# Moving an integer addition from GpSimd to VectorE, and twelve subtractions the other way, in the weight conversion of a fused attention and two-layer kernel

## The chip, the cores and the metric

One NeuronCore of a Trainium2 chip runs the whole program in one launch. The metric is device time in microseconds (us) for one execution, the median of several executions. The engines are TensorE (PE for its matmuls, PEld for its weight loads), VectorE (DVE), ScalarE (ACT), GpSimd (POOL) and SyncE (SP), whose queue issues most of the DMAs.

## The reference

For 8 batches and 8 heads, keys and values are averaged over groups of 8 positions (576 positions become 72), and q (576 x 64 for each head) attends to them. The result, 4608 tokens of 512, passes through two layers. Everything is float32, but the weights arrive as float64.

```
k_p = k.reshape(B, H, S // 8, 8, D).mean(axis=3);  v_p = v.reshape(B, H, S // 8, 8, D).mean(axis=3)
attn = softmax(q @ k_p.T / sqrt(D));  x = attn @ v_p          # 4608 x 512
x = ((x @ w1) * (x @ w2)) @ w3 @ w_out                        # 512 -> 1024 -> 1024 -> 512
h = x @ w_in;  out = (h * sigmoid(1.702 h)) @ w_out2          # 512 -> 2048 -> 512
```

## The kernel before, in words

**Precision.** TensorE works on float32 tiles that are split in two: a rounded part ("hi", a copy by ScalarE, L104) and the rest ("lo", the difference of the value and hi, L105). `split` (L103) makes both; its argument `lo_eng` names the engine of the subtraction, VectorE or GpSimd. Each product is made by three matmuls (`mm3`, L114 to L116): hi by hi, hi by lo, lo by hi.

**Weight conversion.** A float64 weight chunk of 128 x 512 values is loaded as pairs of 32-bit words (512 KB, SP queue, L151). The class `Conv` turns a chunk into float32. `load` (L146) keeps up to nine loaded chunks staged, as slots come free. `step` (L155) takes one: ScalarE turns the high words into `e` (L166) and the low words into small integers (L168, in place), VectorE shifts `e` left by three bits into the tile `cv` (L169), and GpSimd adds the small integers to it as 32-bit integers (L172). Then the slot of the loaded chunk is given back. A line of two further places lets a chunk be used one or two steps later: `turn` transposes w3's chunks on TensorE (L508, into PSUM), and `done` splits the float32 chunk into a slot. `Conv.to` (L139) is `done` for w_out, w1 and w2; without an engine its subtraction goes to GpSimd (L142). w3's chunks are split from PSUM by VectorE (L515).

**First part of the program** (some 110 us). w3 @ w_out is multiplied beforehand, so that the first layer has one matrix in their place. The loop at L568 makes 28 conversion steps: 8 chunks of w_out and 16 of w3, and the first chunks of w1 and w2. Beside them run `w3_mm` (the products, accumulated in PSUM tiles `acc`) and `tick`, which makes one step of the attention of one pair of heads: the transposes of k and q on VectorE (L255, L256), the scores on TensorE (L278), maxima, exponents and sums (L283 to L303: among them L301, an addition of a constant to 128 x 10 values, and L303, the multiplication of 128 x 720 exponents), further transposes (L314 on VectorE), and pooled values and subtractions on GpSimd (L324 to L372). L391 subtracts for the lo part of the attention's output.

**Second part**: nine blocks of 512 tokens (L602), each with eight chunks of 128 hidden values. For each, 24 matmuls make the two products with w1 and w2 in the PSUM tiles `wk`, L638 and L641 (L644 in the last two blocks) multiply them, the product is split, and `x2_step` (L585) multiplies earlier chunks with the combined matrix. Two ticks of attention run in each chunk of seven of the blocks. In the first block the rest of w1 and w2 is converted; in the last two blocks w_in and w_out2 are converted (32 chunks; `e` lies in PSUM here, L616), split by `units` (L463), and written to DRAM.

**Third part** (from about 760 us): the second layer, its weights streamed from DRAM. No conversion runs there.

The order of the instructions on an engine isn't that of the program text: the framework's scheduler sets it when the program is built (`schedule_with_timeline_sim=True` in the launch). Each engine then takes its own list in order, with semaphores between engines.

The change touches `step` at L172, the loop at L551 that names the engine for w_out's chunks (VectorE for the even ones), and L561, which names VectorE for w2's chunks. w1's chunks go to GpSimd already (L559).

Of the kernel before, what the change touches and what calls it, by code (L numbers as in the profile page):

```python
# [22 lines left out]
def pooled_attention_moe_moe2(  # L23
# [18 lines left out]
    nc = tc.nc  # L42
# [6 lines left out]
    w1, w2, w3, w_out, w_in2, w_out2 = (w.bitcast(U32) for w in (w1, w2, w3, w_out, w_in2, w_out2))  # L49
# [45 lines left out]
    def give(*ts):  # L95
        for t in ts:
            if id(t) in held:
                free.append(held.pop(id(t))[1:])
# [19 lines left out]
    def col_tile(w, f):  # L118
        return w[:, 2 * f * P:2 * (f + 1) * P].rearrange("(c p) m -> p c m", p=P)

    def row_tile(w, f):
        return w[f * P:(f + 1) * P, :]
# [4 lines left out]
    class Conv:  # L127
# [27 lines left out]
        def step(self):  # L155

            new = None
            if self.staged:
                t, turn, done = self.staged.pop(0)
                lo_w, hi_w = t[:, :, 0], t[:, :, 1]  # L160
                w = cv_p[0].tile([P, T], F32, name="cv", tag="cv", bufs=4)
                wu = w.bitcast(U32)

                e = self.ps[self.n % len(self.ps)] if self.ps else w
                self.n += 1
                nc.scalar.activation(  # L166
                    e, hi_w.bitcast(F32), AF.Prelu, scale=2.0 ** -112, alpha=-2.0 ** 32)
                nc.scalar.activation(lo_w.bitcast(I32), lo_w, AF.Copy, scale=2.0 ** -29)  # L168
                nc.vector.tensor_scalar(  # L169
                    out=wu, in0=e.bitcast(U32), scalar1=3, scalar2=None,  # L170
                    op0=ALU.logical_shift_left)
                nc.gpsimd.tensor_tensor(  # L172
                    out=w.bitcast(I32), in0=w.bitcast(I32), in1=lo_w.bitcast(I32), op=ALU.add)
                give(t)
                new = [w, turn, done]
            mid, old = self.line
            if mid and mid[1]:
                mid[0] = mid[1](mid[0])
            key = old[2](old[0]) if old else None
            self.line = [new, mid]  # L180
            self.load()
            return key
# [4 lines left out]
    conv = Conv()  # L187
# [3 lines left out]
    with pa_ctx:  # L191
# [264 lines left out]
        wo_s, wp_s, w1_s, w2_s = {}, {}, {}, {}  # L456
# [87 lines left out]
        def add_3(it, jh):  # L544
            conv.add(w3[sl(it), 2 * jh * T:2 * (jh + 1) * T], w3_turn(it, jh), w3_done(it, jh))

        for jh in range(2):
            for i in range(4):
                j = jh * 4 + i
                conv.add(row_tile(w_out, j), None,  # L550
                         conv.to(wo_s, j, nc.gpsimd if i % 2 else nc.vector, j,  # L551
                                 j if j < NA else None))
                if i < 2:
                    add_3(i, jh)
# [3 lines left out]
        for f in range(NF1):  # L558
            conv.add(col_tile(w1, f), None,  # L559
                     conv.to(w1_s, f, a=f - FA if 0 <= f - FA < NA else None))  # L560
            conv.add(col_tile(w2, f), None, conv.to(w2_s, f, nc.vector))  # L561

        conv.load()
        g_load(0)
# [564 lines left out]
```

## Time and profile before

| | us |
|---|---|
| median of 3 executions | 1483.03 (1482.06 to 1484.38) |
| the profiled execution | 1482.22 |
| its span in the profile | 1480.3 |
| PE busy in the span | 1437.6 |
| DVE busy | 989.9 |
| ACT busy | 694.3 |
| POOL busy | 491.0 |

The span runs from the first to the last instruction that the profile shows; 1.9 us of the profiled execution lie around it. A busy share is an average over parts of the program with different limits, so the stretches are looked at one by one. "Granted clock" is the share of TensorE's full clock that the chip gave it. A row of a group reads: line, engine, operation, output tile <- input tiles, shapes, count, then the busy time in us and the mean of one instruction in ns, then idle time of the engine just before and what ended it. A row of a stretch reads: from and to, length, then for PE, PEld, DVE, ACT and POOL the busy time and in brackets the count of instructions, then the granted clock, the mean busy share of the 16 DMA engines and their GB/s.

### The profile page before, as it was taken

What the parts mean: (1) busy time and instruction counts of PE and PEld (TensorE: products, weight loads), DVE (VectorE), ACT (ScalarE), POOL (GpSimd) and SP (SyncE); (2) the same over time, 40 slices, a digit from 0 to 9 for tenths busy, and PEclk for the clock granted to TensorE, in tenths of its full rate; (3) what the DMA queues carried; (4) which work ended last, traced back from release to release, by engine and by line L of the source; (5) the groups of instructions that cost most, each with busy time, mean ns of one, the idle gap of its engine ahead of it and who ended that gap; (6) DMA issues with size and microseconds to landing.
All of it is one profiled execution on the core that took longest, in us unless ns stands there. A gap on an engine that the chain in (4) does not pass through costs nothing.

```text
span 1480.3 us, 19432 instructions
## 1 busy us (share of the span) xinstructions
PE 1437.6 (97%) x6536; PEld 1186.8 (80%) x6536; DVE 989.9 (67%) x1728; ACT 694.3 (47%) x1212; POOL 491.0 (33%) x589
## 2 busy tenths in 40 slices
PE   5978999999999999999999999999999999999998
PEld 3757888888888888888888887788788888888886
DVE  7889998878787877645536355693559354944554
ACT  6874444434343434366635335552455244634442
POOL 8787865555555555357743200000000000000000
PEclk8999999999999999999999999999999999999999
DMA  9992333323232321089879979867677766785665
GB/s 273 235 232 45 65 77 65 74 49 75 48 75 49 74 44 38 29 288 339 329 232 384 336 237 314 295 200 228 199 237 224 223 199 217 240 237 181 194 213 139
DMA packets 294435, 267.64 MB, mean 181 GB/s; under 512 B 201664, under 2 KB 226240, under 8 KB 294336
## 3 DMA queue, kind: packets, MB, share of 16 engines
q1 hardware_dynamic: 291648, 265.09, 59.8%
q10 hardware_dynamic: 2688, 1.31, 0.3%
q8 instruction: 52, 0.85, 0.2%
q14 instruction: 47, 0.39, 0.1%
HBM read 209.72 MB, written 56.62 MB: 180 GB/s over the span
## 4 chain that ended last, share of the span: by engine, by line
PE 85%; DVE 6%; DMA 4%; ACT 3%; issue 1%; SPq 0%; POOL 0%; DVEq 0%; ACTq 0%; POOLq 0%
PE bk L709 40%; PE wk L114 9%; PE wk L116 8%; PE wk L115 8%; PE acc L116 4%; PE acc L114 4%; PE acc L115 4%; PE wk L278 2%; DMA wud<-wt 2%; PE bk L115 1%; PE bk L116 1%; PE bk L114 1%; DVE s L105 1%; DVE cv L169 1%; DMA st<-wind 1%
## 5 line engine op out<-in xcount | busy, mean ns | idle before, releaser
L709 PE MATMUL bk<-mv,st 128*128 128x512 f32 x1152 | 271.5, 389 | 1.0 <-ACT mv L104 1.0
L709 PE MATMUL bk<-xM,st 128*128 128x512 f32 x1092 | 258.5, 390 | 3.2 <-ACT u L967 1.3
L709 PEld LDWEIGHTS bk<-mv,st 128*128 128x128 f32 x1152 | 216.1, 188 | 46.4 <-ACT mv L104 1.6
L709 PEld LDWEIGHTS bk<-xM,st 128*128 128x128 f32 x1092 | 204.5, 188 | 47.6 <-issue 2.5
L114 PE MATMUL wk<-s,s 128*128 128x512 f32 x576 | 227.9, 397 | 6.2 <-DVE a L641 3.6
L115 PE MATMUL wk<-s,s 128*128 128x512 f32 x576 | 225.4, 392 | 1.6 <-DVE s L391 1.5
L116 PE MATMUL wk<-s,s 128*128 128x512 f32 x576 | 225.3, 392 | 0.1
L314 DVE STREAM_TRANSPOSE p<-s_t 32x160 f32<-32x160 f32 (+1 forms) x560 | 178.5, 319 | 10.5
L115 PE MATMUL acc<-s,s 128*128 128x512 f32 x352 | 140.3, 399 | 1.2 <-POOL s L105 1.1
L116 PE MATMUL acc<-s,s 128*128 128x512 f32 x352 | 139.8, 397 | 1.6 <-DVE s L105 1.6
L114 PE MATMUL acc<-s,s 128*128 128x512 f32 x352 | 132.4, 402 | 7.4 <-DVE s L105 5.0
L114 PEld LDWEIGHTS wk<-s,s 128*128 128x128 f32 x576 | 108.7, 189 | 30.5 <-DVE a L641 4.7
L115 PEld LDWEIGHTS wk<-s,s 128*128 128x128 f32 x576 | 108.5, 188 | 24.0 <-DVE s L391 2.4
L116 PEld LDWEIGHTS wk<-s,s 128*128 128x128 f32 x576 | 108.5, 188 | 23.1 <-DVE s L105 0.5
L105 POOL TENSOR_TENSOR s<-a,s 128x512 fp32r<-128x512 f32 x56 | 73.4, 1310 | 155.1 <-ACT s L104 121.3
L105 DVE TENSOR_TENSOR mv<-g,mv 128x1024 fp32r<-128x1024 f32 x80 | 97.7, 1221 | 33.4 <-ACT mv L104 32.1
L104 ACT CAST mv<-g 128x1024 fp32r<-128x1024 f32 x80 | 84.3, 1053 | 72.5 <-PE bk L709 72.1
L172 POOL TENSOR_TENSOR cv<-cv,s 128x512 int32<-128x512 int32 x72 | 100.7, 1406 | 35.9 <-DVE cv L169 22.7
L114 PEld LDWEIGHTS acc<-s,s 128*128 128x128 f32 x352 | 67.2, 192 | 22.5 <-ACT s L104 4.6
L116 PEld LDWEIGHTS acc<-s,s 128*128 128x128 f32 x352 | 67.2, 191 | 15.7 <-DVE s L105 2.9
L115 PEld LDWEIGHTS acc<-s,s 128*128 128x128 f32 x352 | 67.3, 191 | 14.5 <-POOL s L105 2.3
L638 ACT COPY a<-wk 128x512 f32<-128x512 f32 x72 | 42.0, 583 | 68.4 <-PE wk L116 68.2
(188 smaller groups left out, 2341.8 us busy)
## 6 DMA issues: line engine op xcount, KB each, us to landing
st<-wud SPq DMA_DIRECT2D x96, 512.0 KB, 4.3
st<-wind SPq DMA_DIRECT2D x66, 512.0 KB, 4.7
st<-wind SPq DMA_DIRECT2D x76, 256.0 KB, 4.0
s<-in_moe_w_dram SPq DMA_DIRECT2D x32, 512.0 KB, 6.5
wind<-s SPq DMA_DIRECT2D x32, 512.0 KB, 5.4
s<-in_moe_w_out_dram SPq DMA_DIRECT2D x24, 512.0 KB, 6.6
kr<-in_k_dram SPq DMA_DIRECT2D x128, 72.0 KB, 2.5
qr<-in_q_dram SPq DMA_DIRECT2D x128, 72.0 KB, 2.5
```

What stands on the lines that cost most here:

```text
L104: nc.scalar.copy(dst[:, 0], src)
L105: lo_eng.tensor_tensor(out=dst[:, 1], in0=src, in1=f32(dst[:, 0]), op=ALU.subtract)
L114: nc.tensor.matmul(o, a[:, 0, a_sl], b[:, 0, b_sl], start=first, stop=False)
L115: nc.tensor.matmul(o, a[:, 0, a_sl], b[:, 1, b_sl], start=False, stop=False)
L116: nc.tensor.matmul(o, a[:, 1, a_sl], b[:, 0, b_sl], start=False, stop=last)
L169: nc.vector.tensor_scalar(out=wu, in0=e.bitcast(U32), scalar1=3, scalar2=None, op0=ALU.logical_shift_left)
L172: nc.gpsimd.tensor_tensor(out=w.bitcast(I32), in0=w.bitcast(I32), in1=lo_w.bitcast(I32), op=ALU.add)
L278: nc.tensor.matmul(sc[half][:, i * KW:(i + 1) * KW], qT[:, sl(tt)], mov, start=True, stop=True)
L314: nc.vector.transpose(out=dst[:, :nt, 32 * c:32 * c + 32], in_=s_t[32 * c:32 * c + 32, :nt, 32 * r:32 * r + 32])
L638: nc.scalar.copy(a, pa_)
L709: nc.tensor.matmul(o, w[:, x, m], b[:, y], start=first and n == 0, stop=last and n == 2, skip_group_check=True)
```

## The change

The addition of a conversion is made by VectorE, right behind its shift. The subtractions for the lo parts of w_out's four even chunks and of w2's eight chunks are made by GpSimd.

```diff
@@ Conv.step
                 nc.vector.tensor_scalar(
                     out=wu, in0=e.bitcast(U32), scalar1=3, scalar2=None,
                     op0=ALU.logical_shift_left)
-                nc.gpsimd.tensor_tensor(
+                nc.vector.tensor_tensor(
                     out=w.bitcast(I32), in0=w.bitcast(I32), in1=lo_w.bitcast(I32), op=ALU.add)
                 give(t)
@@ conv.add of w_out
             conv.add(row_tile(w_out, j), None,
-                         conv.to(wo_s, j, nc.gpsimd if i % 2 else nc.vector, j,
+                         conv.to(wo_s, j, nc.gpsimd, j,
                                  j if j < NA else None))
@@ conv.add of w2
-            conv.add(col_tile(w2, f), None, conv.to(w2_s, f, nc.vector))
+            conv.add(col_tile(w2, f), None, conv.to(w2_s, f))
```

## Rows read from the trace of the kernel before

**Rows 1.** Busy time by stretch: PE, PEld, DVE, ACT, POOL; clock; DMA share; GB/s

```profile
0.00:20.00 20.00, 9.21 (x25) 6.17 (x26) 11.37 (x16) 15.54 (x26) 13.52 (x22) 1.00 0.94 281
20.00:40.00 20.00, 14.27 (x55) 9.39 (x54) 18.60 (x23) 12.27 (x27) 18.68 (x21) 0.74 1.03 272
40.00:80.00 40.00, 38.37 (x218) 31.48 (x216) 33.50 (x59) 36.80 (x78) 28.66 (x30) 1.00 0.96 227
80.00:120.00 40.00, 30.30 (x128) 22.93 (x129) 35.93 (x52) 28.30 (x63) 33.95 (x41) 0.91 0.99 208
120.00:160.00 40.00, 36.44 (x168) 29.69 (x167) 34.00 (x71) 18.71 (x38) 34.17 (x36) 1.00 0.15 32
160.00:620.00 460.00, 459.45 (x2212) 387.50 (x2212) 379.08 (x931) 183.16 (x414) 247.59 (x357) 1.00 0.26 57
620.00:760.00 140.00, 139.97 (x620) 115.49 (x619) 73.07 (x105) 80.01 (x143) 90.84 (x72) 1.00 0.84 299
760.00:1481.00 721.00, 709.58 (x3120) 584.11 (x3118) 404.38 (x477) 319.53 (x425) 23.59 (x16) 1.00 0.74 235
```

**Rows 2.** What PE waited for, 0 to 160 us: total us, times, longest

```profile
PE wk L508 <- POOL cv L172: 10.6, 2, 9.2
PE acc L114 <- DVE s L105: 5.0, 3, 3.0
PE wk L114 <- DVE a L641: 3.6, 2, 1.9
PE wk L278 <- DVE qT L256: 2.8, 2, 2.1
...
PE acc L116 <- DVE s L105: 1.6, 1, 1.6
PE wk L115 <- DVE s L391: 1.5, 1, 1.5
```

**Rows 3.** Groups by line and shape, VectorE, 0 to 160 us

```profile
L169 DVE TENSOR_SCALAR cv<-cv 128x512 uint32<-128x512 uint32 x40 | 30.8, 777 | 10.5 <-ACT cv L166 10.5
L105 DVE TENSOR_TENSOR s<-cv,s 128x512 fp32r<-128x512 f32 x11 | 13.1, 1187 | 1.5 <-ACT s L104 1.5
...
L301 DVE TENSOR_SCALAR nm<-nm 128x10 f32<-128x10 f32 x7 | 8.9, 1271 | 0.1
L303 DVE TENSOR_TENSOR s_t<-s_t,nm 128x720 f32<-128x720 f32 x4 | 8.0, 1988 | 0.1
```

**Rows 4.** Groups by line and shape, GpSimd, 0 to 160 us

```profile
L172 POOL TENSOR_TENSOR cv<-cv,s 128x512 int32<-128x512 int32 x40 | 54.9, 1377 | 17.3 <-DVE cv L169 4.3 <-DMA s<-in_moe_w_dram 3.5 <-DMA kr<-in_k_dram 1.9
L105 POOL TENSOR_TENSOR s<-cv,s 128x512 fp32r<-128x512 f32 x12 | 15.5, 1295 | 3.0 <-ACT s L104 2.8
```

**Rows 5.** Single lines over the whole span: ns min/median/max, first and last start

```profile
L169 DVE TENSOR_SCALAR cv<-cv x40: 357/515/2590, 5.5 to 148.9; 128x512 uint32<-128x512 uint32 x40
...
L301 DVE TENSOR_SCALAR nm<-nm x32: 155/173/3399, 30.8 to 610.8; 128x10 f32<-128x10 f32 x32
...
L303 DVE TENSOR_TENSOR s_t<-s_t,nm x30: 895/899/4380, 33.9 to 611.2; 128x720 f32<-128x720 f32 x30
...
L105 DVE TENSOR_TENSOR s<-cv,s x12: 679/1146/2070, 8.1 to 169.6; 128x512 fp32r<-128x512 f32 x12
```

**Rows 6.** Timeline of GpSimd, 5 to 11 us: start, us, instruction

```profile
7.84 1.30 POOL L172 TENSOR_TENSOR cv<-cv,s 128x512 int32<-128x512 int32 x1 [0.42 <-DVE cv L169]
```

**Rows 7.** Timeline of VectorE, 30 to 36 and 82 to 91 us

```profile
30.75 2.25 DVE L301 TENSOR_SCALAR nm<-nm 128x10 f32<-128x10 f32 x1
...
83.51 3.40 DVE L301 TENSOR_SCALAR nm<-nm 128x10 f32<-128x10 f32 x1
```

**Rows 8.** Timeline of GpSimd, 83 to 88 us

```profile
85.60 1.27 POOL L172 TENSOR_TENSOR cv<-cv,s 128x512 int32<-128x512 int32 x1
```

**Rows 9.** Busy time of line 172 alone (GpSimd), 40 to 80 us

```profile
40.00:80.00 40.00, 14.41 (x11) 1.00 0.96 227
```

**Rows 10.** Groups by line and shape, GpSimd, 620 to 760 us

```profile
L172 POOL TENSOR_TENSOR cv<-cv,s 128x512 int32<-128x512 int32 x32 | 45.7, 1442 | 18.7 <-DVE cv L169 18.4
```

## The prediction, made before the change was run

> **What bounds the kernel now.** I read the stretches first. In each, the reader should subtract PE's busy time from the length: from 160 to 760 us PE is idle for 0.6 us, from 760 on for 11.4 us with no conversion running, and from 0 to 160 us for 31.4 us [rows 1]. All later time is PE's own work, so what the change does from 160 us on is seen only if it makes PE idle there; what it does before 160 us shifts the end one for one. The conversions lie in two places: 40 before 160 us, 32 from 620 to 760 us [rows 4, 10].
>
> Next, the waits of PE before 160 us. VectorE ends five kinds of them, 14.5 us in nine waits; GpSimd's addition ends 10.6 us, of which 9.2 is the start of the program [rows 2]. So VectorE sets the pace more than GpSimd. Both are crowded: VectorE is busy 133.4 of 160 us, GpSimd 129.0, and loads keep the DMA engines at 0.94 to 1.03 until 120 us [rows 1].
>
> Last, what fills VectorE. The shift takes 0.36 us at best and 0.78 on the mean; L301 0.16 against 1.27; L303 0.90 against 1.99; the subtraction from `cv` 0.68 against 1.19 [rows 3, 5]. One L301 of 3.40 us on 128 x 10 values ends at 86.91, 0.04 after a GpSimd addition (85.60 plus 1.27) [rows 7, 8]. I read this as VectorE being held while GpSimd runs. For the 40 shifts the surplus is 30.8 - 40 x 0.36 = 16.4 us, for seven L301 8.9 - 1.1 = 7.8, for four L303 8.0 - 3.6 = 4.4: 28.6 us of VectorE's time are waiting [rows 3, 5].
>
> **The change part by part, up to 160 us.**
>
> *GpSimd* loses 54.9 us of additions and gains twelve subtractions, at 1.295 us each 15.5 us: 129.0 becomes 89.6 us, 81% becomes 56% [rows 1, 4].
>
> *VectorE gains* 40 additions. No row shows one on VectorE; the nearest is the subtraction from `cv`, same size, two SBUF inputs: 0.68 us free, 1.19 us on the mean as now held [rows 3, 5]. I take 0.88, which is 0.68 plus half of the 0.41 that a shift loses now, because GpSimd is less full then: 35.2 us, ends 27.2 and 47.6.
>
> *VectorE loses* eleven subtractions before 160 us, 13.1 us [rows 3]; the twelfth starts at 169.6 [rows 5].
>
> *VectorE is held less.* If the surplus follows GpSimd's busy share, it falls by 30%: 8.7 us. If VectorE must find a gap between GpSimd's instructions, it follows busy over free time (129/31 against 89.6/70.4) and falls by 69%: 19.8 us. The L301 of 3.40 us is longer than any single GpSimd instruction that the groups show (means of 1.3 to 1.4), so it outlasted several; I take the middle, 14.3 us [rows 4, 7].
>
> The Trainium skill ("SBUF — State Buffer", Who interferes with whom) says that the engine which starts first holds the shared port pair for its whole instruction. By that, a wait should end with one GpSimd instruction, the relief would be the 8.7 us, and VectorE would gain 13.4 us where the next sentence has 7.8; the 3.40 us row does not agree.
>
> Net: 35.2 - 13.1 - 14.3 = 7.8 us more on VectorE, ends -5.7 (27.2 - 13.1 - 19.8) and +25.8 (47.6 - 13.1 - 8.7). It has 26.6 us idle in this stretch [rows 1], so most of it needn't show; what counts is what PE waits for:
>
> (a) The start. The first transposes wait 9.2 us; the last link is a GpSimd addition of 1.30 us that began 0.42 us after GpSimd could have gone on [rows 2, 6]. On VectorE 0.68 takes its place: -0.6, and up to -1.1 if the shift ahead of it is not held. I take -0.8.
> (b) The other 10.6 - 9.2 = 1.4 us of waiting for an addition: half goes, -0.7 [rows 2].
> (c) PE's one wait of 1.6 us for a subtraction [rows 2]: I put it at the L301 of 2.25 us from 30.75 [rows 7], 2.1 of it surplus. -1.5.
> (d) PE's wait of 1.5 us for L391 [rows 2], which I put behind the 3.40 us L301: an addition of 1.27 us leaves the run that held it [rows 8]. -1.3.
> (e) Two waits for L641, 3.6 us [rows 2]; one L303 grew to 4.38 us [rows 5]. I give half of one: -0.9.
> (f) Against it, 40 to 80 us. Eleven additions run there [rows 9] and VectorE has 6.5 us idle [rows 1]: 11 x 0.88 = 9.7 less about 2 us of relief is 7.7, 1.2 over. With something for order, +1.5.
>
> Sum: -0.8 - 0.7 - 1.5 - 1.3 - 0.9 + 1.5 = -3.7 us.
>
> *The new wait.* VectorE's addition needs ScalarE's low words; GpSimd waited for them before. Behind it VectorE's whole list waits. Nearest row: shifts waited 10.5 us for ScalarE in all [rows 3]. As the low words are made while the shift runs, I take 0; the upper end is another 10.5 us of waiting on VectorE, which its 26.6 us of idle time may absorb or not. No DMA is moved; SP's load only waits for the slot, which the shorter addition frees sooner.
>
> *The twelve subtractions* cost 0.1 us more each on GpSimd; the 39.4 us that GpSimd loses hide it. Without this cover it is 1.2 us.
>
> *From 620 to 760 us* 32 additions, 45.7 us, leave GpSimd [rows 10] and 22 to 38 us (0.68 to 1.19 each) come to VectorE, which is busy 73.1 of 140. PE is idle for 0.03 us [rows 1]: no gain is possible, and 67 us of free VectorE time hide the cost. If that cover failed at each of the 16 token chunks by half an addition, it would be 16 x 0.35 = 5.6 us. I take 0. *After 760 us* nothing changes.
>
> The profiled execution took 1482.2 us, 1.9 more than its span; -3.7 gives 1478.5. The median of the three runs lies 0.8 above, so 1479.3 stands against it.
>
> **The rivals.**
>
> *Slower: one more VectorE instruction ahead of every piece PE waits for.* VectorE ends nine of PE's waits [rows 2]; it is already 93% busy from 20 to 40 and 90% from 80 to 120 us [rows 1]. If each of the nine pieces gets one addition of 0.88 us ahead of it, that is +7.9; (c) to (e) are then eaten up, (a) and (b) stay, (f) stays: 7.9 - 1.5 + 1.5 = +7.9, or 1490.9. It decides as soon as five of the nine are hit (4.4 against 3.7). For it: VectorE is the engine that PE waits for. Against it: the longest VectorE instructions are waits for the engine that is relieved.
>
> *No change: the loads set the pace.* Until 120 us the DMA engines are 0.94 to 1.03 busy [rows 1], and the loaded bytes don't change; what engines save, they wait for chunks, and what they lose was slack. Then only (a) at the start and some of (e) after 120 us are left, and against these the additions: within 3 us of 1483. Against it: PE's list of waits has no load among those that I read, and GB/s falls from 281 to 208 while the share stays [rows 1, 2]. The additions bring a second road to it: held as the shifts are now, they lose up to 0.5 each, 40 x 0.5 = 20 us, against 14.3 us of relief, so that the waiting only changes sides. The Trainium skill ("Perfetto Trace Analysis", Optimizing Scalar/DVE Operations) warns that shifting work between these two engines might not help, as they share a read port; that is this rival's second road, and no row here shows an addition on VectorE that could confirm it.
>
> *That the change doesn't do what it says* I exclude: the lines name the engines.
>
> **How the numbers follow.** 0.2%, 3 us, is about what a measurement of this kernel tells from no change. Forecast (faster): 0.42; no change: 0.28; slower: 0.30. The forecast's own range is 1473 to 1480: the low end has (a) to (e) in full, -1.1 - 1.4 - 1.6 - 1.5 - 3.6 = -9.2 without (f). The granted clock from 20 to 40 us is 0.74 on the mean, a mix of 1.2 and 2.4 GHz, behind a stretch in which PE was busy for 9.2 of 20 us [rows 1]; fewer gaps may better it, which I don't price, since PE still waits there. The range that should hold 8 in 10 reaches from 1472.5 to the slower rival's 1491; beyond it lie the 25.8 us end and the late cover's failure.
>
> **What would show it.** Right: L172 on VectorE at 0.7 to 1.0 us on the mean; shifts well below 0.78; L301 near 0.2 to 0.6; GpSimd near 90 us before 160 us; VectorE near 141; PE's idle time before 160 us near 28 us, the first transposes before 8.6 us, 620 to 760 us still without gaps. Wrong: additions above 1.1 us, shifts still at 0.7, more waits of PE for VectorE; or the same idle time with PE or ScalarE waiting for loads. A wait for ScalarE's low words in front of the additions would show the new wait.

## The result, and the profile after

The changed kernel takes **1499.96 us** (median of 5 runs, 1497.07 to 1500.96) where the kernel before takes 1483.03 (1480.11 to 1485.14): the ratio is 1.0111, with a 95% interval of [1.0097, 1.0126]. It is 17 us slower; the forecast was 4 us faster. The profiled execution took 1497.07 us, its span is 1495.3, against 1482.22 and 1480.3; it is the fastest of the five, and its granted clock the highest (0.991 on the mean of the span, the others 0.984 to 0.987). The first part of the page shows the busy time of each engine in the span:

```profile
PE 1439.4 (96%) x6536; PEld 1188.9 (80%) x6536; DVE 1022.3 (68%) x1788; ACT 695.6 (47%) x1212; POOL 410.3 (27%) x529
```

PE's own work is 1.8 us longer than before (1437.6). So of the 15.0 us that the span grew, about 13 are idle time of PE. The busy time by stretch says where; the columns are those of [rows 1]:

```profile
0.00:20.00 20.00, 10.18 (x36) 7.41 (x36) 13.50 (x22) 15.45 (x26) 8.47 (x18) 1.00 0.92 282
20.00:40.00 20.00, 13.42 (x60) 9.51 (x61) 18.80 (x29) 13.87 (x30) 10.30 (x14) 0.83 1.00 268
40.00:80.00 40.00, 34.25 (x177) 28.08 (x176) 32.31 (x59) 28.88 (x61) 12.70 (x19) 0.96 0.82 210
80.00:120.00 40.00, 30.43 (x140) 23.34 (x138) 35.82 (x52) 33.11 (x74) 31.10 (x37) 0.87 0.93 212
120.00:160.00 40.00, 31.67 (x137) 24.34 (x136) 39.12 (x79) 16.19 (x35) 28.90 (x38) 1.00 0.22 45
160.00:620.00 460.00, 456.29 (x2192) 385.33 (x2193) 375.22 (x908) 184.26 (x414) 245.12 (x348) 1.00 0.27 58
620.00:760.00 140.00, 138.54 (x618) 114.26 (x618) 96.76 (x157) 79.84 (x146) 45.73 (x41) 1.00 0.76 276
```

Set against [rows 1], PE is 1.0 us busier in the first 20 us, and loses 0.9 from 20 to 40, 4.1 from 40 to 80, 4.8 from 120 to 160, 3.2 from 160 to 620 and 1.4 from 620 to 760. Its idle time before 160 us is 40.1 us instead of 31.4. GpSimd was relieved as planned (0 to 160 us: 91.5 us instead of 129.0) and VectorE is 6.2 us fuller (139.6 instead of 133.4). Nor are the DMA engines at their limit where PE loses: from 40 to 80 us they are less busy than before (0.82 against 0.96), and from 120 to 160 us 0.22.

What PE waited for from 0 to 160 us (total us, times, longest), to be read against [rows 2]:

```profile
PE wk L508 <- DVE cv L172: 9.9, 2, 7.9
PE acc L114 <- ACT s L104: 4.3, 3, 1.9
PE wk L380 <- DVE s_t L285: 3.2, 1, 3.2
PE acc L380 <- DVE s L285: 3.0, 1, 3.0
PE wk L278 <- ACT kbd L261: 2.9, 2, 2.4
PE acc L114 <- DVE s L105: 2.8, 2, 2.4
PE wk L278 <- DVE qT L256: 2.0, 1, 2.0
PE wk L114 <- DVE a L641: 1.9, 3, 1.3
...
PE wk L278 <- DVE s L391: 1.4, 1, 1.4
PE wk L115 <- DVE s L391: 1.0, 1, 1.0
...
```

The wait for the addition at the start is 1.2 us shorter (the first transposes begin at 7.95 us instead of 9.19), and those for L105 (acc L114, 5.0) and L641 (3.6) shrank. New ones have come: 6.2 us for attention's L285 and 2.9 for ScalarE's `kbd` (L261); that for ScalarE's copies (L104) was 2.4 before. The waits for L391 are 2.4 us together (1.5 before). The groups of VectorE from 0 to 160 us stand against [rows 3]:

```profile
L172 DVE CUSTOM_DVE_ANT_0 cv<-s,cv 128x1024 uint16<-128x1024 uint16 x40 | 34.9, 876 | 1.4 <-ACT s L168 0.2
L169 DVE TENSOR_SCALAR cv<-cv 128x512 uint32<-128x512 uint32 x40 | 27.5, 692 | 8.7 <-ACT cv L166 8.5
...
L301 DVE TENSOR_SCALAR nm<-nm 128x10 f32<-128x10 f32 x6 | 6.5, 1086 | 0.0
L303 DVE TENSOR_TENSOR s_t<-s_t,nm 128x720 f32<-128x720 f32 x4 | 5.6, 1400 | 0.0
```

The forty additions cost 34.9 us, where 35.2 were forecast. Shifts, L301 and four L303 together are 8.1 us shorter (47.7 became 39.6; L301 runs six times here instead of seven); 14.3 were forecast. So VectorE's total came out nearly as predicted, though one of its terms did not, and PE lost 8.6 us before 160 us all the same. The next question is what in the program changed besides the engines.

### The profile page after: what moved, and what is told of

It reads as the page before. It is cut to its first block, busy times and chain, and to the rows that moved or that the text cites. A ratio compares the mean times of both kernels' runs of the same rounds, so it can differ in the third digit from the quotient of the medians.

```text
span 1495.3 us, 19394 instructions
## 1 busy us (share of the span) xinstructions
PE 1439.4 (96%) x6536; PEld 1188.9 (80%) x6536; DVE 1022.3 (68%) x1788; ACT 695.6 (47%) x1212; POOL 410.3 (27%) x529
## 3 DMA queue, kind: packets, MB, share of 16 engines
q10 hardware_dynamic: 2688, 1.31, 0.3%
## 4 chain that ended last, share of the span: by engine, by line
PE 80%; DMA 8%; DVE 7%; SPq 2%; ACT 2%; issue 1%; ACTq 0%; DVEq 0%
PE bk L709 38%; PE wk L114 8%; PE wk L115 8%; PE wk L116 8%; PE acc L115 4%; PE acc L116 4%; PE acc L114 4%; DMA s<-in_moe_w_dram 3%; DMA wud<-wt 2%; PE wk L278 2%; SPq L229 1%; DVE p L314 1%; DVE cv L172 1%; PE bk L114 1%; PE bk L115 1%
## 5 line engine op out<-in xcount | busy, mean ns | idle before, releaser
L114 PE MATMUL wk<-s,s 128*128 128x512 f32 x576 | 228.2, 397 | 4.9 <-DVE a L641 1.9
L115 PE MATMUL wk<-s,s 128*128 128x512 f32 x576 | 225.2, 392 | 3.4 <-DVE s L391 3.4
L116 PE MATMUL wk<-s,s 128*128 128x512 f32 x576 | 224.9, 391 | 0.0
L116 PE MATMUL acc<-s,s 128*128 128x512 f32 x352 | 140.3, 399 | 0.1
L114 PE MATMUL acc<-s,s 128*128 128x512 f32 x352 | 133.0, 402 | 7.3 <-ACT s L104 4.5
L115 PE MATMUL acc<-s,s 128*128 128x512 f32 x352 | 139.5, 396 | 0.0
L114 PEld LDWEIGHTS wk<-s,s 128*128 128x128 f32 x576 | 108.6, 189 | 29.7 <-DVE a L641 3.0
L115 PEld LDWEIGHTS wk<-s,s 128*128 128x128 f32 x576 | 108.6, 189 | 25.8 <-DVE s L391 4.3
L116 PEld LDWEIGHTS wk<-s,s 128*128 128x128 f32 x576 | 108.4, 188 | 22.7
L105 DVE TENSOR_TENSOR mv<-g,mv 128x1024 fp32r<-128x1024 f32 x80 | 97.7, 1222 | 32.9 <-ACT mv L104 31.5
L104 ACT CAST mv<-g 128x1024 fp32r<-128x1024 f32 x80 | 84.2, 1053 | 71.9 <-PE bk L709 71.4
L105 POOL TENSOR_TENSOR s<-a,s 128x512 fp32r<-128x512 f32 x56 | 72.4, 1292 | 160.1 <-ACT s L104 126.1
L114 PEld LDWEIGHTS acc<-s,s 128*128 128x128 f32 x352 | 67.8, 193 | 21.6 <-ACT s L104 6.0
L116 PEld LDWEIGHTS acc<-s,s 128*128 128x128 f32 x352 | 67.3, 191 | 14.2 <-DVE s L105 1.2
L115 PEld LDWEIGHTS acc<-s,s 128*128 128x128 f32 x352 | 67.5, 192 | 12.6
L981 DVE TENSOR_TENSOR g<-bk,u 128x512 f32<-128x512 f32 x32 | 22.1, 690 | 66.8 <-PE bk L709 66.8
```

What stands on the lines that cost most here:

```text
L104: nc.scalar.copy(dst[:, 0], src)
L105: lo_eng.tensor_tensor(out=dst[:, 1], in0=src, in1=f32(dst[:, 0]), op=ALU.subtract)
L114: nc.tensor.matmul(o, a[:, 0, a_sl], b[:, 0, b_sl], start=first, stop=False)
L115: nc.tensor.matmul(o, a[:, 0, a_sl], b[:, 1, b_sl], start=False, stop=False)
L116: nc.tensor.matmul(o, a[:, 1, a_sl], b[:, 0, b_sl], start=False, stop=last)
L981: nc.vector.tensor_tensor(out=g12[:, i], in0=o, in1=U[i], op=ALU.add)
```

## The experiments

**Two kinds of difference.** The scheduler that sets each engine's list at build answered the change with other lists. A comparison of the two built programs shows hundreds of instructions in another place, the largest part on PE, and some on each of DVE, ACT, POOL and SP; 40 plus 32 moved additions and twelve moved subtractions account for few of them, and on PE for none. The first difference on PE, right at the start (- before, + after):

```
 L115 MATMUL acc_66<-s_192,s_202 128x512
+L508 MATMUL wk_71<-ident,cv 128x128 x4
 L116 MATMUL acc_66<-s_192,s_202 128x512
 L114 MATMUL acc_66<-s_216,s_202 128x512
-L508 MATMUL wk_71<-ident,cv 128x128 x4
```

Two theories follow. *The moved work*: VectorE's list carries forty additions more before 160 us, and PE waits behind them. *The new order*: the lists as the scheduler rewrote them cost the time, whatever engine adds. The experiments first take the change apart, then hold the order.

### Half of the change at a time

**Additions alone** (subtractions as before):

```diff
-                nc.gpsimd.tensor_tensor(
+                nc.vector.tensor_tensor(
                     out=w.bitcast(I32), in0=w.bitcast(I32), in1=lo_w.bitcast(I32), op=ALU.add)
```

> All 72 additions on VectorE; the twelve subtractions stay where they were before (w_out's even chunks and w2 on VectorE). Theory 1 (VectorE is too full before 160 us): 12 subtractions of 0.7 to 1.2 us more on VectorE than in the changed kernel, so at least as slow, 1499 to 1508. Theory 2 (the new order of the instructions and of the loads behind one another on SP's queue costs the time, not VectorE's load): no fixed relation to the changed kernel, 1485 to 1505. Theory 3 (GpSimd's twelve subtractions cost the time, as they come late there): back near 1483.

Measured: 1492.86 us (1490.38 to 1499.92), against 1483.25 for the kernel before beside it; 1.0073 [1.0050, 1.0095].

**Subtractions alone** (additions on GpSimd):

```diff
-                         conv.to(wo_s, j, nc.gpsimd if i % 2 else nc.vector, j,
+                         conv.to(wo_s, j, nc.gpsimd, j,
...
-            conv.add(col_tile(w2, f), None, conv.to(w2_s, f, nc.vector))
+            conv.add(col_tile(w2, f), None, conv.to(w2_s, f))
```

> Only the twelve subtractions go to GpSimd; the additions stay on GpSimd. Theory 1: VectorE loses 13 us before 160 us, so 1476 to 1484. Theory 2: another order of the loads, so a change of several us either way. Theory 3: slower, 1490 or more, as GpSimd is then 90% busy.

Measured: 1498.79 us; 1.0108 [1.0086, 1.0131]. Twelve subtractions of some 1.3 us moved to another engine, no addition touched, cost as much as the whole change. The halves, +0.7% and +1.1%, do not add up to its +1.1%. Costs that belonged to the instructions would be expected to, unless they hide one another.

**The two places of the additions.** In the next two, only the early forty, or only the late 32, are on VectorE (`self.ps` is set for the late ones); the first of them has the subtractions of the change, the second those of before.

```diff
-                nc.vector.tensor_tensor(
+                (nc.gpsimd if self.ps else nc.vector).tensor_tensor(
```

> As the changed kernel, but the 32 additions of w_in and w_out2 (from 620 us on) stay on GpSimd. Theory 1: the loss lies before 200 us; PE's missing 1.4 us between 740 and 760 us come back: 1497 to 1500, against 1500 for the changed kernel. If the late conversions cost more than the trace shows, 1495 or less.

> As before, but the 32 late additions go to VectorE, which has 67 us free there. Theory 1: 1483 to 1485 (1.4 us at 740 to 760 us at most). If the late conversions carry the loss: 1488 or more.

Measured: early forty with the subtractions 1496.33 us, 1.0086 [1.0060, 1.0112]; late 32 alone 1484.56 us, 1.0005 [0.9994, 1.0016]. The early part carries most of the loss. The late one is free within the 0.2% that can be told, though it left a gap in its profiled execution; what PE waited for there from 620 to 760 us:

```profile
PE wk L114 <- DVE s L105: 2.4, 1, 2.4
```

The changed kernel shows the same wait with 1.3 us.

### The order held

A kernel can be given another's order: between neighbours of the wanted list of an engine an edge is added that only the scheduler sees (no semaphore and no wait of the chip comes with it). Instructions that stand on that engine in one kernel alone, the moved ones, are left for the scheduler to place.

```diff
+    for engine, names in json.loads(zlib.decompress(base64.b85decode(_ORDER))).items():
+        last = None
+        for n in names:
+            ins = by_name.get(f"I-{n}")
...
+            if last is not None:
+                tc.add_manual_dep(ins, last.name, info, reason="pin_order")
+            last = ins
```

**The changed kernel in the order of before, and the kernel before in the order of the changed one**, on all five engines:

> The changed kernel's engines, but every instruction that stayed on its engine is issued in the order of the kernel before, on all five engines; only the 72 additions and twelve subtractions are put in by the scheduler, on their new engines. Theory 1 (the moved work itself costs the time: VectorE fuller, GpSimd's subtractions later): still slow, 1495 to 1503. Theory 2 (the scheduler wrote a worse order for TensorE, the loads and the rest): back to 1478 to 1486.

> The kernel before with its own engines for additions and subtractions, but every other instruction in the order of the changed kernel. Theory 1: near 1483, up to 1488. Theory 2: 1492 to 1503, the order carries the loss.

Measured, with the kernel before at 1482.68 beside them (the changed kernel's ratio is that of the result above):

| ratio to the kernel before | order of before | order of the changed kernel |
|---|---|---|
| engines of before | 1 | 1.0121 [1.0104, 1.0138], 1501.07 us |
| engines of the changed kernel | 1.0030 [1.0019, 1.0041], 1486.72 us | 1.0111 [1.0097, 1.0126], 1499.96 us |

Across a row only the order changes: +18 us with the engines of before, and about +12 (0.81% of 1483) with those of the change. Down a column only the engines change: +4 us in the old order, -1.5 in the new one, with intervals that overlap. The order is the larger cause in either row.

Not all that the order costs is idle time. In the profiled execution of the kernel before in the new order (span 1502.2 us, 21.9 more than before) PE is idle for 31.6 us before 160 us, hardly more than before (31.4), but its busy time in the whole span is 1449.0 us instead of 1437.6, for the same matmuls. Its granted clock is lower; two of its stretches, to be read against 0.91 and 1.00 in [rows 1]:

```profile
80.00:120.00 40.00, 31.99 (x128) 25.29 (x128) 25.84 (x46) 30.46 (x72) 33.89 (x40) 0.79 0.84 173
120.00:160.00 40.00, 36.75 (x157) 29.82 (x156) 37.33 (x76) 18.00 (x35) 35.37 (x43) 0.91 0.21 45
```

From 95 to 100 us, for example, PE was busy for 1.95 of 5 us, and the granted clock of the next 5 us was 0.53, near the lower of its two levels (1.2 of 2.4 GHz). So about half of that execution's loss is matmuls that took longer. That all 11.4 us come from the clock is not shown.

The stretches of the changed kernel in the order of before:

```profile
0.00:20.00 20.00, 9.89 (x33) 6.58 (x34) 13.41 (x22) 15.29 (x26) 8.22 (x18) 1.00 0.93 282
20.00:40.00 20.00, 14.35 (x71) 10.91 (x69) 19.18 (x31) 15.34 (x33) 12.53 (x15) 0.91 1.05 276
40.00:80.00 40.00, 35.30 (x194) 28.79 (x192) 35.65 (x68) 32.69 (x69) 14.16 (x17) 0.98 0.92 237
80.00:120.00 40.00, 31.52 (x135) 25.39 (x135) 33.77 (x57) 30.19 (x68) 30.27 (x40) 0.85 0.95 195
120.00:160.00 40.00, 32.00 (x131) 25.71 (x130) 37.84 (x67) 15.49 (x31) 25.40 (x28) 0.92 0.11 23
160.00:620.00 460.00, 459.45 (x2217) 387.74 (x2216) 375.69 (x919) 183.75 (x414) 248.07 (x356) 1.00 0.27 58
620.00:760.00 140.00, 140.00 (x623) 116.10 (x623) 95.29 (x152) 82.66 (x149) 50.15 (x43) 1.00 0.82 290
```

From 160 to 760 us PE is full again: 0.6 us idle, as in [rows 1], where the changed kernel has 5.2 (3.7 and 1.5). So that loss comes with the order. One place of it can be read in the changed kernel on VectorE's timeline:

```profile
200.81 6.34 DVE L314 STREAM_TRANSPOSE p<-s_t 32x160 f32<-32x160 f32 x19
207.18 0.33 DVE L391 TENSOR_TENSOR s<-wk,s 128x160 fp32r<-128x160 f32 x1
```

Nineteen of a tick's twenty transposes stand ahead of L391, for which PE waits 2.5 us. In the kernel before, this tick is the fifth from 120 us on, and there the same L391 stands ahead of all twenty:

```profile
195.71 0.32 DVE L391 TENSOR_TENSOR s<-wk,s 128x160 fp32r<-128x160 f32 x1
196.46 2.63 DVE L314 STREAM_TRANSPOSE p<-s_t 32x160 f32<-32x160 f32 x8
```

The kernel before in the new order has that wait too. What PE waited for from 160 to 620 us there:

```profile
PE wk L115 <- DVE s L391: 2.4, 1, 2.4
```

**Where the remaining 4 us are.** Before 160 us the changed kernel in the old order has PE idle for 36.9 us, 5.5 more than before: +0.7 and +0.1 in the first two stretches, -3.1 from 40 to 80, +1.2 from 80 to 120, -4.4 from 120 to 160 us (after 760 us it is idle for 1.9 us less). The last shows how an addition costs PE time. VectorE from 147 to 160 us (start, us, instruction):

```profile
150.47 0.55 DVE L169 TENSOR_SCALAR cv<-cv 128x512 uint32<-128x512 uint32 x1
151.06 5.14 DVE L172 CUSTOM_DVE_ANT_0 cv<-s,cv 128x1024 uint16<-128x1024 uint16 x1
156.12 0.68 DVE L391 TENSOR_TENSOR s<-wk,s 128x288 fp32r<-128x288 f32 x2
```

GpSimd in the same microseconds:

```profile
151.21 0.73 POOL L324 TENSOR_TENSOR va<-vr 128x256 f32<-128x256 f32 x1
151.91 2.52 POOL L105 TENSOR_TENSOR s<-cv,s 128x512 fp32r<-128x512 f32 x2
154.40 1.25 POOL L105 TENSOR_TENSOR s<-a,s 128x512 fp32r<-128x512 f32 x1
155.61 1.16 POOL L324 TENSOR_TENSOR vat<-vtr 32x256 f32<-32x256 f32 x1
```

And PE:

```profile
156.62 1.80 PE L278 MATMUL wk<-kbd,qT 128*128 128x144 f32 x6 [2.77 <-DVE s L391]
```

An addition that takes 0.69 us elsewhere took 5.14, through four GpSimd instructions that followed one another without a gap; the L324 then running took 1.16 us, where its like at 121.55 us took 0.73. L391 stood behind the addition, and PE waited 2.77 us for it. A second addition, from 119.61 us, took 4.48, and PE later waited 3.31 us for L641. All forty together took more than in the changed kernel, the shifts less:

```profile
L172 DVE CUSTOM_DVE_ANT_0 cv<-s,cv 128x1024 uint16<-128x1024 uint16 x40 | 41.0, 1027 | 1.3
L169 DVE TENSOR_SCALAR cv<-cv 128x512 uint32<-128x512 uint32 x40 | 22.8, 572 | 7.2 <-ACT cv L166 7.2
...
L303 DVE TENSOR_TENSOR s_t<-s_t,nm 128x720 f32<-128x720 f32 x4 | 5.9, 1484 | 0.0
L301 DVE TENSOR_SCALAR nm<-nm 128x10 f32<-128x10 f32 x6 | 4.8, 793 | 0.0
```

**Each half in the order of before:**

> Only the twelve subtractions on GpSimd, the rest in the order of before. Theory 1: near the 1499 of the same move with a free order, as GpSimd's lo halves come late. Theory 2: 1478 to 1488.

> Only the 72 additions on VectorE, the rest in the order of before. Theory 1: 1490 to 1500. Theory 2: 1478 to 1486.

Measured: subtractions alone 1484.86 us, 1.0017 [1.0002, 1.0032]; additions alone 1484.09, 1.0009 [0.9996, 1.0022]. With the scheduler's own orders the same two were 1.0108 and 1.0073: of each half's cost, too, the order had the greater part. And now the halves do add up: 2.2 + 1.4 = 3.6 us, against 4.0 for both, though each is known to some 2 us only. Without the twelve subtractions on GpSimd the additions take 0.87 us on the mean and the longest 1.83; the two long ones above are held for 8.2 us. But the hold at 151 us is there without them too, on a subtraction that stayed on VectorE:

```profile
150.97 4.03 DVE L105 TENSOR_TENSOR s<-cv,s 128x512 fp32r<-128x512 f32 x1
```

GpSimd's run beside it holds two subtractions where it holds three above, and the hold is 1.1 us shorter.

### Is any new order worse, or this one?

Two kernels change engines without moving work: of the subtractions, w_out's odd and even chunks are swapped, or w1's and w2's.

```diff
-                         conv.to(wo_s, j, nc.gpsimd if i % 2 else nc.vector, j,
+                         conv.to(wo_s, j, nc.vector if i % 2 else nc.gpsimd, j,
```

> The kernel before with the engines of w_out's subtractions swapped: the odd chunks on VectorE, the even ones on GpSimd. Each engine does as much work as before; only the order that the scheduler writes is new. If its order is what the time hangs on: more than 4 us away from 1483, either way. If the kernel before is no special case: 1480 to 1487.

```diff
-                     conv.to(w1_s, f, a=f - FA if 0 <= f - FA < NA else None))
-            conv.add(col_tile(w2, f), None, conv.to(w2_s, f, nc.vector))
+                     conv.to(w1_s, f, nc.vector, a=f - FA if 0 <= f - FA < NA else None))
+            conv.add(col_tile(w2, f), None, conv.to(w2_s, f))
```

> The kernel before with w1's subtractions on VectorE and w2's on GpSimd: equal work again, a new order from the first chunk of w1 on. If the order is what the time hangs on: more than 4 us from 1483. If not: 1480 to 1487.

Measured, with the kernel before at 1483.73: 1491.3 us, 1.0048 [1.0030, 1.0066], and 1487.88, 1.0021 [1.0011, 1.0031]. With equal work what comes out is 4 and 8 us slower than before. These two were not run in the order of before, so it is not shown how much of that is the order and how much the other choice of chunks. Nor is it proof that every new order is worse, since the late additions alone gave one that is not.

### Which engine's list?

In the changed kernel, some lists are put into the order of before, and the scheduler sets the others. SyncE's alone was suspected, since its queue waited 19.8 us for the transposes of k and q up to 170 us (L229 for L255 and L256; 6.9 before), and ScalarE waited longer for weight chunks (17.7 us up to 160 us, 5.7 before). TensorE's alone is the other.

> The changed kernel with SP's queue alone in the order of before, the other engines ordered anew. If the loss lies in the loads standing behind one another on SP's queue: 1484 to 1490. If it lies in the order of the engines: 1494 or more.

> The changed kernel with TensorE alone in the order of before, the other queues ordered anew around it. If the loss lies in the order of TensorE's matmuls: 1484 to 1490. If it lies in the loads or in VectorE's order: 1494 or more.

Measured: SyncE's 1497.98 us, 1.0090 [1.0075, 1.0105]; TensorE's 1509.33, 1.0162 [1.0145, 1.0179]. Up to 160 us SyncE's waits fell from 13.2 to 7.0 us, but one of 28.9 us ends just behind it, so that up to 170 us they rose from 19.8 to 36.0; the time hardly moved. So this run did not take these waits away, but their length doesn't set the time: in the first of the two sets below they are 44.5 us, and it is faster. With TensorE's old list alone it becomes worse than with either full order. Then in sets:

> The changed kernel with TensorE's, ScalarE's and SyncE's lists in the order of the kernel before, VectorE's and GpSimd's lists as the scheduler of the changed kernel has them. If the loss is carried by the order of PE, ACT and SP, it comes near the kernel with all five lists restored: 1486 to 1490. If it is carried by VectorE's and GpSimd's lists, it stays at 1496 to 1500. If the lists only serve one another (each order good only together with the others, as TensorE's alone gave 1509 and SyncE's alone 1498), it is no better than the changed kernel: 1497 or more.

> The changed kernel with VectorE's, ScalarE's and GpSimd's lists in the order of the kernel before, TensorE's and SyncE's lists as the scheduler of the changed kernel has them. If the loss is carried by the elementwise engines' lists, it comes near the kernel with all five lists restored: 1486 to 1490. If it is carried by PE and SP, it stays at 1496 to 1500. If the lists only serve one another, it is 1497 or more, as the other part's kernel.

Measured, with the kernel before at 1482.42: the first 1492.56 us, 1.0062 [1.0045, 1.0079]; the second 1496.01, 1.0079 [1.0057, 1.0102]. Against the changed kernel's 1.0111, TensorE's list alone loses some 8 us, TensorE's with ScalarE's and SyncE's gain 7, the other set gains 5 (the intervals just overlap), and all five gain 12; neither set reaches the 1.0030 of all. So neither set holds the loss by itself, and the two gains add up. TensorE's old list by itself costs time, and together with ScalarE's and SyncE's it saves some: 1509.33 against 1492.56. The lists of VectorE, ScalarE and GpSimd were not tried one by one. Which pairs of instructions matter most stays open, beyond the place shown at 207 us, and so does which matmuls ran at the lower clock because of it. No kernel tried was faster than the one before.

## Why the prediction was wrong, point by point

**The step that failed** is the sum over (a) to (f). It took PE's waits one by one from [rows 2] and changed the length of the instruction in front of each, as if the lists stayed as they were; yet a scheduler sets them at build. All that the sum had for order was some 0.3 us in (f), and no rival held a term for it. The runs put 12 to 18 us on it, where the sum was -3.7 and the range reached +8. And with the order held the sum was wrong too: the moved work cost 4.0 us (1486.72 against 1482.68), for the reasons that follow.

**VectorE's account was right in its total, by luck, and wrong in what it is worth.** Its busy time before 160 us was to become 141 and became 139.6 (139.8 in the old order); GpSimd's was to become 90 and became 91.5. An addition was priced at 0.88 us and took 0.876 (1.027 in the old order). With 34.9 us of additions, 13.1 of subtractions gone and 8.1 of relief, VectorE should have gained 13.7 us, not 6.2; the rest is mostly attention that no longer got done by 160 us (L255 nine times instead of ten, L301 six instead of seven). The relief was put at 14.3 us. In the old order it is 14.2: shifts 30.8 - 22.8 = 8.0, L301 8.9 - 4.8 = 4.1, four L303 8.0 - 5.9 = 2.1, against [rows 3]; in the new order 8.1. One L301 fewer is in both; counted by the instruction, the old order's relief is 13.0. But the additions were held themselves: 40 x (1.027 - 0.69) = 13.5 us in the old order, 40 x (0.876 - 0.69) = 7.4 in the new. The waiting changed sides, which is the second road of the rival "no change". The Trainium skill ("Perfetto Trace Analysis", Optimizing Scalar/DVE Operations) warns that moving work between these two engines might not help, and these 13.5 us against 13.0 to 14.2 agree with it. That rival's first road, loads that set the pace, did not hold: the DMA share was 0.82 and 0.22 in the two stretches where PE lost most, and in the kernel before in the new order, as slow as the changed one, ScalarE waited for weight chunks for 7.5 us up to 160 us, against 5.7 before.

**How a hold ends.** The prediction let a wait outlast several GpSimd instructions, on the strength of a single row [rows 7]. The 5.14 us addition beside four GpSimd instructions, of 0.73, twice 1.26 and 1.25 us, shows it plainly. The Trainium skill ("SBUF — State Buffer", Who interferes with whom) says that the engine which issues first has the shared pair of ports for its whole instruction. The prediction took this to mean that a wait ends with that one instruction; so read, the addition should have lost 1.3 us at the most, and it lost 4.4. The measurement decides.

**(a)** was right in direction: the start's wait fell from 9.19 to 7.95 us, 1.2 where 0.8 was forecast and 1.1 the most, and the first transposes began at 7.95 us, before the 8.6 that was named as a sign. **(b)** In the old order the 1.4 us are gone, in the new one 2.0 remain. **(c)** went in the new order, which has no wait of acc L116 for a subtraction; in the old one 1.0 of 1.6 us remain. **(d)** did not come true: the wait of L115 for L391 is 1.0 instead of 1.5, but L278 waits another 1.4 for an L391. Its cure failed in the old order as well, where PE waited 2.77 us for another L391 behind a held addition. **(e)** L641's 3.6 us became 1.9 in the new order and 5.2 in the old. **(f)** was +1.5 and is 3.1 in the old order and 4.1 in the new: it was sized at less than half. The stretch from 120 to 160 us, 4.4 to 4.8 us, had no term against the change at all.

**The new wait** for ScalarE's low words was rightly taken at 0: 0.2 us. **The twelve subtractions** were costed at 0.1 us each and hidden; on top of the moved additions they cost some 2.6 us in the old order (1486.72 against 1484.09, with intervals that overlap). The hold of 5.14 us shows how they can: two of the four GpSimd instructions beside it are subtractions from `cv`, where the additions alone have one there and a hold of 4.03 us; before 160 us GpSimd makes 22 such subtractions, where it made 12 [rows 4]. **The late additions** at 0 were right within what can be told (1.0005), though the cover shows a hole of 1.3 to 2.4 us in the scheduler's orders and none in the old.

**The slower rival** ended on the right side, with 7.9 us for nine waited pieces that get one addition ahead. Its mechanism is real, as the chain addition, L391, PE shows, but in the old order, where it can be seen by itself, all that the change moves costs 4 us. Executions of the kernel before alone lie between 1478.1 and 1487.2 us over all the series, so terms of about 1 us, as (a) to (f) were, can't be told apart in the total.

## What to carry to other kernels

Where a scheduler orders the instructions at build, a change of engine is two changes, and the second can be the larger: compare the built lists, and price an order that was found good as something that can be lost (here 12 to 18 us with this change; with equal work, and the order not held, 4 and 8). Hold the old order when you measure a move, so that its own cost can be seen. Look at the granted clock beside the idle time, since a new order can cost through both. And before moving work to an engine that is held beside the one it comes from, subtract from the relief the same wait for what you move.

## What was not expected of the hardware

The addition of 32-bit integers on VectorE does not run as the integer TENSOR_TENSOR that GpSimd ran [rows 4], but as a custom instruction on 128 x 1024 16-bit values, 0.69 us at the median for 128 x 512 words (0.64 at best), against GpSimd's 1.31. Undisturbed it costs no more than a float32 subtraction of the size (0.68 at best [rows 5]), and it is held beside a busy GpSimd up to 5.14 us.
